# One block of quarter-array products per unit, from the sixth unit on, in a fused recurrence and feed-forward kernel

## The chip, the cores and the metric

The kernel runs on one core of one Trainium2 chip. The metric is the time of one execution on the device, in microseconds (us), as the median of separate runs. A profile of one more execution shows what each engine did: PE is TensorE's matmuls (PEld its weight loads), DVE is VectorE, ACT is ScalarE, POOL is GpSimd and SP is the engine that issues most DMAs.

## The reference

A gated linear recurrence over 768 tokens for 4 batches and 8 heads of 48, whose output is the input of a feed-forward layer (384 to 2048 to 384, with ELU between):

```
f = 1.0 / (1.0 + np.exp(-f_logit))
for t in range(S):
    state = f[:, :, t, :, None] * state + np.einsum('bhd,bhe->bhde', k[:, :, t], v[:, :, t])
    y[:, :, t] = np.einsum('bhd,bhde->bhe', q[:, :, t], state)
x = y.transpose(0, 2, 1, 3).reshape(B * S, H * D)          # (3072, 384)
h = x @ w_in                                               # (3072, 2048)
g = np.where(h > 0.0, h, np.exp(np.minimum(h, 0.0)) - 1.0)
out = g @ w_out                                            # (3072, 384)
```

All arithmetic is float32.

## The kernel before

**Units and stages.** The 3072 tokens are cut into 12 units of 256 tokens (three to a batch), numbered 0 to 11. A unit passes through the recurrence first and through the feed-forward layer a stage later. From unit 2 on, a stage is the time in which one unit's feed-forward layer runs. It has 20 steps, and `base(m)` is the number of the first one of unit m's stage. I write "step 8 of stage 6" for `base(6) + 8`. One pass of the main loop handles two steps, with the loop counter `s`.

**The order is written out by hand.** `at_step(T, ...)` puts functions into a plan, and the main loop calls them at step T. Within one pass the loop calls the plan's functions of the even step, then issues two phases of the feed-forward layer, then the vector joins that belong to them, then the plan's functions of the odd step, then the activations of a finished quad, and last some down products (`take`). Each engine works through its own instructions in exactly that order, so a function's place in the plan fixes what stands behind it on every engine that it uses.

**The feed-forward layer.** A unit's 16 column blocks of `w_in` are four quads. A quad is five phases, i = 0 to 4, of 3, 5, 5, 4 and 3 full-array products into two PSUM banks (`psH`, "side 0" and "side 1"; the next quad's side 0 lies in the bank of this quad's side 1). ACT copies the phases' results to `vals` (L988), and after phase 1 it writes one block back into the bank (L990, the seed), onto which phase 3 adds. DVE's joins (L972, `joins`) finish a quad: JOIN3 reads side 1, JOIN4 reads side 0, MID and LAST stay in SBUF. Then ACT makes the exponentials (L996, L997), DVE the ELU (L1016, `elu`), POOL four sums (L1029). The down products (L1080, `down`) take these into four PSUM banks `psM`, tags m0 to m3, which hold a whole unit. When a unit's last down product is done, ACT copies one bank half (L1091) and DVE makes five adds (L1090) that write the output tile; these are the closing adds, and they free m3, m0, m1 and m2 in that order. The unit's end falls at the end of step 7 of the next stage.

**The recurrence of unit u.** `load` fetches f, k, q, v. `gates` (ACT, two activations L673 and L675) makes the gate's denominator. For each of three pairs of heads `grow` (DVE scan, L687) and `fall` (DVE reciprocal, L692) make the running decay, and `scale` (POOL) multiplies k and q by it. `transposed` turns k on the PE. Then come four groups of quarter-array products, each of 64 x 64 (or 64 x 48) with four of them side by side in the array, 32 products a group (24 in the carried part of a batch's first unit):

- `advance`: the states' increments (psU, L806); DVE adds them up in `step` (L764, one for each of 4 chunks),
- `scores`: q times k (psS, L783); DVE multiplies them by a mask in `mask` (L791),
- `outputs`: masked scores times v (psY, L821),
- `carried`: q times the states, added onto the same psY (L845); then ACT copies psY to the unit's x tile (L852, L854).

For a unit u these stand in the stage of unit u-1 (`t = base(u - 1)`): transposes at step 3, advance and scores at step 9 (`both`), outputs at step 12, carried at step 13. `advance` writes banks a0 and a1, `scores` m3 and m0, and `outputs` a0 and a1. So a stage has three separate blocks of quarter-array products among the full-array ones. The decays of the unit after that stand at steps 1, 5 and 15 of a stage, its gates at step 19 (`D6`, and `t - 21`).

A weight check, spread over the run, rereads w_in and w_out by DMA (`reread`) and passes them through ACT (`check`, L665 and L666).

Of the kernel before, what the change touches and what calls it, by code (L numbers as in the profile page):

```python
# [356 lines left out]
def fast(ctx: ExitStack, tc: tile.TileContext, q, k, v, f_logit, w_in, w_out, out, flag, outer):  # L357
# [53 lines left out]
    D6 = (-19, -15, -5, 1)  # L411
    A3 = (3, 9, 12, 13)
    BL = 16
    BL2 = 29
# [380 lines left out]

    def advance(u, pairs=range(HP)):

        if u not in pus:
            pus[u] = [ps.tile([128, NW, HP, D], FP32, tag=n, name=f"psU{u}_{n}") for n in ("a0", "a1")]
        pu = pus[u]  # L800
        for p in pairs:
            for w in range(NW):
                for r in range(2):
                    h = 2 * p + r
                    for b in range(2):
                        nc.tensor.matmul(  # L806
                            pu[b][FULL[r], w, p], lhsT=kn[FULL[b], p, w, FULL[r]],
                            rhs=vs[u % NB][FULL[b], w, PAD + h * D : PAD + (h + 1) * D],
                            start=(w == 0 and p == 0), stop=(w == NW - 1 and p == HP - 1), skip_group_check=True,
                        )  # L810
# [23 lines left out]
    def carried(u):  # L834

        t = qkf[u % NB]
        py = pys.pop(u)
        for w in range(NW):
            for p in range(HP):
                for b in range(2):  # L840
# [3 lines left out]
                    for r in range(2):  # L844
# [3 lines left out]
                            start=False, stop=True, skip_group_check=True,  # L848
                        )
        x = x_tile(u)  # L850
        to = x[:, 0:HP].rearrange("n p (w b i) -> n b w p i", b=2, i=C)
# [68 lines left out]
    def attention(u, first, then):  # L920
# [12 lines left out]
        if u > 1:  # L933
            at_step(then[-2], lambda: outputs(u))
        at_step(then[-1], lambda: carried(u))

# [96 lines left out]
    def down(P):  # L1033
# [28 lines left out]
        else:  # L1062
# [6 lines left out]
            if j == plain and m < NU - 1:  # L1069
                todo = todo[2:5] + todo[:2] + todo[5:]  # L1070
            if j >= NP - 1 - (m == NU - 1):
                todo = todo[:3] + todo[5:6] + todo[3:5] + todo[6:]
# [187 lines left out]
    for u in range(3, NU):  # L1260
        t = base(u - 1)
        for n in range(6):
            at_step(t + BL + n // 5 * 2, lambda u=u, n=n: blend(u, nc.gpsimd, slice(n, n + 1)))
        at_step(base(u - 2) - (0, 3, 6)[min(u - 3, 2)], lambda u=u: load(u))
        at_step(t - (11, 19, 21)[min(u - 3, 2)], lambda u=u: gates(u))
        attention(u, [t + i for i in (D3, D4, D5, D6)[min(u - 3, 3)]], [t + i for i in A3])
    for n in range(NR):
# [139 lines left out]
```

## Time and profile before

| | us |
|---|---|
| median of 3 runs | 548.81 |
| lowest and highest | 548.62, 551.91 |
| profiled execution, first to last instruction | 549.1 |
| one steady stage of 20 steps (306.34 to 348.31) | 41.97 |
| PE busy in the profiled execution | 532.8 |
| DVE, POOL, ACT busy | 407.3, 338.2, 317.2 |

The profiled execution's own time is its span, 549.1 us; it lies 0.3 us above the median of the runs. A PE product of float32 appears in the trace as two rows, so a group of 32 products is "x64" and a phase of 3 products is "x6". The distance between the starts of two groups is the time that a group takes, since a row's own duration overlaps the next one.

### The profile page before, as it was taken

What the parts mean: (1) busy time and instruction counts of PE and PEld (TensorE: products, weight loads), DVE (VectorE), ACT (ScalarE), POOL (GpSimd) and SP (SyncE); (2) the same over time, 40 slices, a digit from 0 to 9 for tenths busy, and PEclk for the clock granted to TensorE, in tenths of its full rate; (3) what the DMA queues carried; (4) which work ended last, traced back from release to release, by engine and by line L of the source; (5) the groups of instructions that cost most, each with busy time, mean ns of one, the idle gap of its engine ahead of it and who ended that gap; (6) DMA issues with size and microseconds to landing.
All of it is one profiled execution on the core that took longest, in us unless ns stands there. A gap on an engine that the chain in (4) does not pass through costs nothing.

```text
span 549.1 us, 15619 instructions
## 1 busy us (share of the span) xinstructions
PE 532.8 (97%) x6302; PEld 497.6 (91%) x6302; DVE 407.3 (74%) x717; ACT 317.2 (58%) x649; POOL 338.2 (62%) x560
## 2 busy tenths in 40 slices
PE   7699899999999999999999999999999999999996
PEld 3577678899999999999999999999999999999995
DVE  8699968875888887687687687777867865654563
ACT  4459773235656467566566566575675574574441
POOL 8230227779798398288388378478568567454452
PEclk9789999999999999999999999999999999999999
DMA  8999961005052271261262252243244212110001
GB/s 202 238 268 254 265 180 44 1 15 139 8 148 73 60 191 41 60 184 49 60 167 66 60 144 88 60 120 112 60 106 126 60 23 87 54 45 2 30 1 38
DMA packets 38964, 53.92 MB, mean 98 GB/s; under 512 B 3904, under 2 KB 28704, under 8 KB 38880
## 3 DMA queue, kind: packets, MB, share of 16 engines
q1 hardware_dynamic: 38464, 52.51, 36.1%
q8 instruction: 52, 0.85, 0.7%
q10 hardware_dynamic: 416, 0.30, 0.2%
q14 instruction: 32, 0.26, 0.2%
HBM read 45.02 MB, written 4.72 MB: 91 GB/s over the span
## 4 chain that ended last, share of the span: by engine, by line
PE 82%; DVE 9%; ACT 4%; issue 2%; DMA 2%; SPq 0%; POOL 0%; DVEq 0%; ACTq 0%; POOLq 0%
PE psM L1080 32%; PE psH L982 29%; PE psH L1006 7%; PE psM L1042 4%; DVE vals L972 3%; PE psY L821 2%; PE psY L845 2%; DVE f L692 2%; PE psU_a L806 2%; PE psS L783 2%; DVE gg L1016 1%; ACT gg L997 1%; ACT gg L996 1%; DMA again<-in_moe_w_out_dram 1%; PE psT L743 1%
## 5 line engine op out<-in xcount | busy, mean ns | idle before, releaser
L1029 POOL TENSOR_TENSOR sums<-gg 128x128 f32<-128x128 f32 x172 | 101.8, 611 | 125.0 <-DVE gg L1016 124.3
L988 ACT COPY vals<-psH 128x512 f32<-128x512 f32 (+1 forms) x120 | 65.5, 545 | 122.4 <-PE psH L982 118.3
L982 PE MATMUL psH<-xt,wi 128*128 128x128 f32 x880 | 131.4, 276 | 0.1
L972 DVE TENSOR_TENSOR vals<-vals,psH 128x256 f32<-128x256 f32 (+1 forms) x160 | 61.8, 386 | 85.3 <-PE psH L982 46.4
L982 PE MATMUL psH<-xt,area 128*128 128x128 f32 x720 | 118.0, 277 | 0.8 <-DVE vals L972 0.6
L982 PEld LDWEIGHTS psH<-xt,wi 128*128 128x128 f32 x880 | 115.2, 192 | 0.8 <-DVE gg L1016 0.3
L1080 PE MATMUL psM<-area,sums 128*128 128x192 f32 x516 | 103.5, 327 | 0.0
L982 PEld LDWEIGHTS psH<-xt,area 128*128 128x128 f32 x720 | 100.9, 191 | 2.2 <-PE psS L783 1.1
L1080 PEld LDWEIGHTS psM<-area,sums 128*128 128x128 f32 x516 | 85.8, 190 | 0.3 <-POOL sums L1029 0.2
L1080 PE MATMUL psM<-wo,gg 128*128 128x192 f32 x376 | 76.7, 329 | 0.0
L1016 DVE SCALAR_TENSOR_TENSOR gg<-gg,vals 128x512 f32<-128x512 f32 x80 | 64.1, 836 | 9.7 <-ACT gg L997 9.7
L972 DVE TENSOR_TENSOR vals<-vals 128x256 f32<-128x256 f32 x120 | 64.4, 551 | 2.0
L682 POOL TENSOR_TENSOR k<-k,f 128x256 f32<-128x256 f32 x48 | 35.8, 749 | 45.3 <-DMA k<-in_k_dram 21.3
L692 DVE RECIPROCAL f<-f 128x256 f32<-128x256 f32 x36 | 62.8, 1748 | 1.0
L1080 PEld LDWEIGHTS psM<-wo,gg 128*128 128x128 f32 x376 | 61.1, 190 | 1.8 <-DVE at L791 1.6
L997 ACT ACTIVATE gg<-gg 128x512 f32<-128x512 f32 x96 | 60.5, 631 | 3.1
L996 ACT ACTIVATE gg<-vals 128x512 f32<-128x512 f32 x80 | 49.5, 619 | 18.1 <-DVE vals L972 18.0
L962 POOL TENSOR_TENSOR xt<-xt 128x256 f32<-128x256 f32 x57 | 48.6, 867 | 3.2 <-DVE xt L962 1.8
L1006 PE MATMUL psH<-xt,wi 128*128 128x256 f32 x192 | 47.3, 398 | 1.7 <-DVE xt L902 1.7
L682 POOL TENSOR_TENSOR q<-q,f 128x256 f32<-128x256 f32 x48 | 40.9, 855 | 12.3 <-ACT f L712 9.4
L1029 POOL TENSOR_TENSOR sums<-sums,gg 128x128 f32<-128x128 f32 x86 | 47.5, 552 | 0.2
L1006 PEld LDWEIGHTS psH<-xt,wi 128*128 128x128 f32 x192 | 37.6, 199 | 8.6 <-DVE xt L902 1.9
(115 smaller groups left out, 751.0 us busy)
## 6 DMA issues: line engine op xcount, KB each, us to landing
area<-in_moe_w_out_dram SPq DMA_DIRECT2D x8, 768.0 KB, 11.6
again<-in_moe_w_in_dram SPq DMA_DIRECT2D x16, 384.0 KB, 4.3
again<-in_moe_w_out_dram SPq DMA_DIRECT2D x16, 384.0 KB, 3.7
k<-in_k_dram SPq DMA_DIRECT2D x12, 384.0 KB, 4.2
q<-in_q_dram SPq DMA_DIRECT2D x12, 384.0 KB, 5.6
v<-in_v_dram SPq DMA_DIRECT2D x12, 384.0 KB, 6.2
area<-in_moe_w_in_dram SPq DMA_DIRECT2D x8, 576.0 KB, 11.7
out_dram<-o SPq DMA_DIRECT2D x42, 96.0 KB, 1.7
```

The source lines that it names most:

```text
L682: e.tensor_tensor(out=t[n][:, p], in0=t[n][:, p], in1=t["f"][:, p, "kq".index(n)], op=ALU.mult)
L692: nc.vector.reciprocal(f[:, p, 1], f[:, p, 0])
L962: e.tensor_tensor(out=pick(x, to), in0=pick(x, a), in1=pick(x, b), op=ALU.subtract)
L972: nc.vector.tensor_tensor(out=pick(v, to), in0=x, in1=y, op=op)
L982: nc.tensor.matmul(bank[:, slot], lhsT=w_block(q, w), rhs=xts[m][:, x], start=(i < 2 and t == 0), stop=True, skip_group_check=True,)
L988: nc.scalar.copy(v[:, at : at + size], bank[:, frm : frm + size])
L996: nc.scalar.activation(g[:], h, AF.Relu, scale=-1.0)
L997: nc.scalar.activation(g[:], g[:], AF.Exp, scale=-1.0)
L1006: nc.tensor.matmul(ph[:, i], lhsT=wi[j][:, kt, i * 128 : (i + 1) * 128], rhs=xts[m][:, 2 * kt : 2 * kt + 2].rearrange("n t f -> n (t f)"), ...
L1016: nc.vector.scalar_tensor_tensor(out=g[:], in0=g[:], scalar=-1.0, in1=phs.pop(P), op0=ALU.add, op1=ALU.max)
L1029: nc.gpsimd.tensor_tensor(out=s[:, i], in0=x, in1=y, op=op)
L1080: nc.tensor.matmul(pm[bank][:, half * DH : (half + 1) * DH], lhsT=x, rhs=y, start=first, stop=(j == NP - 1), skip_group_check=True,)
```

## The change

From unit 5 (`DEEP`) on, the recurrence is planned by `deep` and not by `attention`. `window(u)`, at step 9 of the stage of unit u-1, issues on the PE without a break `outputs(u)`, `scores(u + 1)`, `advance(u + 1)` and `carried(u)`, and then, for DVE, `mask(u + 1)` and the steps of u + 1. So scores and states are made one unit earlier than before. `advance` writes m1 and m2 there, and `scores` m3 and m0. The copies of psY to x become `placed_x` and stand two steps later. The transposes of u + 1, the gates and the decays of later units move a stage earlier, to other steps: from unit 7 on the loads of f and k to step 2, the gates to step 6, the first decay to step 8, the second to step 12, the third to step 16. Unit 5 gets advance and scores by themselves in stage 3. The first seven down products of a unit are issued in another order.

```diff
+    DEEP = 5
+    D_DEEP = ((2, 5, 8, 13), (-5, -4, -2, 1), (-12, -8, -4, 1))
...
-    def advance(u, pairs=range(HP)):
+    def advance(u, pairs=range(HP), banks=("a0", "a1")):
...
     def carried(u):
...
-        py = pys.pop(u)
+        py = pys[u]
...
+    def placed_x(u):
+
+        py = pys.pop(u)
         x = x_tile(u)
...
-        at_step(then[-1], lambda: carried(u))
+        at_step(then[-1], lambda: carried(u), lambda: placed_x(u))
+
+    def window(u):
+
+        outputs(u)
+        if u + 1 == NU:
+            carried(u)
+            return
+        pc = scores(u + 1, ("m3", "m0"))
+        advance(u + 1, banks=("m1", "m2"))
+        carried(u)
+        mask(u + 1, pc)
+        for c in range(NC):
+            step(u + 1, c)
+
+    def deep(u):
+
+        t, kept = base(u - 2), []
+        d = [t + i for i in D_DEEP[min(u - DEEP, 2)]]
+        for p in range(NKT):
+            at_step(d[p], lambda p=p: grow(u, p), lambda p=p: fall(u, p), lambda p=p: scale(u, ("k", p, nc.gpsimd)))
+        at_step(d[NKT - 1], lambda: move(u, slice(0, 2), nc.sync))
+        for p in range(NKT):
+            at_step(d[p + 1] if u == DEEP else t + ((-1, 0, 1) if u == DEEP + 1 else (-3, -1, 1))[p], lambda p=p: scale(u, ("q", p, nc.gpsimd)))
+        at_step(d[NKT], lambda: watch(u), lambda: scale(u, ("k", NKT, nc.gpsimd), ("q", NKT, nc.gpsimd)))
+        at = t + (15 if u == DEEP else 3)
+        at_step(at, lambda: transposed(u, 0, "a0"), lambda: transposed(u, 1, "a1"))
+        if u == DEEP:
+            at_step(at + 2, lambda: advance(u), *(lambda c=c: step(u, c) for c in range(NC)))
+            at_step(at + 3, lambda: kept.append(scores(u)), lambda: mask(u, kept[0]))
+        at_step(base(u - 1) + A3[1], lambda: window(u))
+        at_step(base(u - 1) + A3[1] + 2, lambda: placed_x(u))
...
             if j == plain and m < NU - 1:
                 todo = todo[2:5] + todo[:2] + todo[5:]
+                if m >= DEEP - 1:
+                    todo = [todo[i] for i in (4, 3, 5, 1, 2, 0, 6)]
...
-        at_step(base(u - 2) - (0, 3, 6)[min(u - 3, 2)], lambda u=u: load(u))
-        at_step(t - (11, 19, 21)[min(u - 3, 2)], lambda u=u: gates(u))
-        attention(u, [t + i for i in (D3, D4, D5, D6)[min(u - 3, 3)]], [t + i for i in A3])
+        if u <= DEEP:
+            at_step(base(u - 2) - (0, 3, 6)[min(u - 3, 2)], lambda u=u: load(u))
+            at_step(t - (11, 19, 21)[min(u - 3, 2)], lambda u=u: gates(u))
+        else:
+            at_step(base(u - 2) - (10 if u == DEEP + 1 else 18), lambda u=u: load(u, "fk"))
+            at_step(base(u - 2) - (6 if u == DEEP + 1 else 10), lambda u=u: load(u, "qv"))
+            at_step(base(u - 2) - (6 if u == DEEP + 1 else 14), lambda u=u: gates(u))
+        if u < DEEP:
+            attention(u, [t + i for i in (D3, D4, D5, D6)[min(u - 3, 3)]], [t + i for i in A3])
+        else:
+            deep(u)
```

What stands where, in stage 6. On ACT, from the exponentials of unit 6's first quad (gg6_0, gg6_1) to the copy of m0 that begins unit 5's closing (u2_5); before:

```order
L996 ACTIVATE gg6_0_3262<-vals0_126 128x512
L997 ACTIVATE gg6_0_3262<-gg6_0_3262 128x512
L996 ACTIVATE gg6_1_3265<-vals0_126 128x512
L997 ACTIVATE gg6_1_3265<-gg6_1_3265 128x512
L665 ACTIVATE again12_3199,spans_140<-again12_3199 128x384
L666 ACTIVATE again12_3199,spans_140<-again12_3199 128x384
L988 COPY vals1_127<-psH6_1_1_3277 128x512
L990 COPY psH6_1_1_3277<-vals1_127 128x128
L988 COPY vals1_127<-psH6_1_0_3252 128x512
L1091 COPY u2_5_3313<-psM5_0_2953 128x192
```

and changed, where the line numbers are some 40 higher:

```order
L1033 ACTIVATE gg6_0_3366<-vals0_126 128x512
L1034 ACTIVATE gg6_0_3366<-gg6_0_3366 128x512
L1033 ACTIVATE gg6_1_3369<-vals0_126 128x512
L1034 ACTIVATE gg6_1_3369<-gg6_1_3369 128x512
L675 ACTIVATE f1_71<-f1_71 128x3x256
L677 ACTIVATE f1_71<-f1_71 128x3x256
L667 ACTIVATE again12_3307,spans_140<-again12_3307 128x384
L668 ACTIVATE again12_3307,spans_140<-again12_3307 128x384
L1025 COPY vals1_127<-psH6_1_1_3383 128x512
L1027 COPY psH6_1_1_3383<-vals1_127 128x128
L1025 COPY vals1_127<-psH6_1_0_3360 128x512
L1130 COPY u2_5_3419<-psM5_0_3130 128x192
```

The two activations of unit 9's gates (f1) have come in ahead of the copies of quad 1 (psH6_1), of the seed and of u2.

On DVE, from unit 5's last closing add (o5) over quad 1's joins to the masks; before:

```order
L1090 TENSOR_TENSOR o5_3312<-psM5_2_2955,u43_5_3314 128x384
L972 TENSOR_TENSOR vals1_127<-vals1_127,psH6_1_1_3277 128x2x128 x2
L972 TENSOR_TENSOR vals1_127<-psH6_1_1_3277,vals1_127 128x128
L972 TENSOR_TENSOR vals1_127<-vals1_127,psH6_1_0_3252 128x2x128
L972 TENSOR_TENSOR vals1_127<-vals1_127,psH6_1_0_3252 128x128
L972 TENSOR_TENSOR vals1_127<-vals1_127 128x2x128
L972 TENSOR_TENSOR vals1_127<-vals1_127 128x256
L972 TENSOR_TENSOR vals1_127<-vals1_127 128x2x128
L791 TENSOR_TENSOR at7_3374<-psS7_0_3375,twice_109 128x512
L791 TENSOR_TENSOR at7_3374<-psS7_1_3376,twice_109 128x512
```

and changed:

```order
L1129 TENSOR_TENSOR o5_3418<-psM5_2_3132,u43_5_3420 128x384
L689 SCALAR_TENSOR_TENSOR f1_71<-f1_71 128x256
L694 RECIPROCAL f1_71<-f1_71 128x256
L1009 TENSOR_TENSOR vals1_127<-vals1_127,psH6_1_1_3383 128x2x128 x2
L1009 TENSOR_TENSOR vals1_127<-psH6_1_1_3383,vals1_127 128x128
L1009 TENSOR_TENSOR vals1_127<-vals1_127,psH6_1_0_3360 128x2x128
L1009 TENSOR_TENSOR vals1_127<-vals1_127,psH6_1_0_3360 128x128
L1009 TENSOR_TENSOR vals1_127<-vals1_127 128x2x128
L1009 TENSOR_TENSOR vals1_127<-vals1_127 128x256
L1009 TENSOR_TENSOR vals1_127<-vals1_127 128x2x128
L793 TENSOR_TENSOR at8_3485<-psS8_0_3486,twice_109 128x512
L793 TENSOR_TENSOR at8_3485<-psS8_1_3487,twice_109 128x512
```

The scan and the reciprocal of unit 9's first decay have come in between the closing adds and quad 1's joins; the masks behind them are unit 8's, not unit 7's.

On the PE, the first down products of unit 6 behind the block; before:

```order
L1080 MATMUL psM6_2_3439<-area_139,gg6_0_3262 128x192
L1080 MATMUL psM6_1_3438<-area_139,sums6_0_3292 128x192 x2
L1080 MATMUL psM6_0_3437<-wo_138,gg6_0_3262 128x192
L1080 MATMUL psM6_3_3440<-wo_138,gg6_0_3262 128x192
L1080 MATMUL psM6_0_3437<-area_139,sums6_0_3292 128x192
```

and changed:

```order
L1119 MATMUL psM6_3_3623<-wo_138,gg6_0_3366 128x192
L1119 MATMUL psM6_0_3620<-wo_138,gg6_0_3366 128x192
L1119 MATMUL psM6_0_3620<-area_139,sums6_0_3398 128x192
L1119 MATMUL psM6_1_3621<-area_139,sums6_0_3398 128x192 x2
L1119 MATMUL psM6_2_3622<-area_139,gg6_0_3366 128x192
```

Before, the first three go to m2 and m1, which hold nothing of the recurrence; changed, all four banks hold scores or increments when these products are due, m3 and m0 until the masks, m1 and m2 until the steps.

More of the change, by code (lines that the diff above doesn't have):

```diff
@@ L794, in mask @@
             )
-    def advance(u, pairs=range(HP)):
+    def advance(u, pairs=range(HP), banks=("a0", "a1")):
         if u not in pus:
-            pus[u] = [ps.tile([128, NW, HP, D], FP32, tag=n, name=f"psU{u}_{n}") for n in ("a0", "a1")]
+            pus[u] = [ps.tile([128, NW, HP, D], FP32, tag=n, name=f"psU{u}_{n}") for n in banks]
         pu = pus[u]
```

## The prediction

> **What bounds the kernel now.** I read the page's busy times and its chain first, then the windows of single stages, then the timelines of PE, ACT and DVE around step 9.
>
> ```profile
> PE 532.8 (97%) x6302; PEld 497.6 (91%) x6302; DVE 407.3 (74%) x717; ACT 317.2 (58%) x649; POOL 338.2 (62%) x560
> PE 82%; DVE 9%; ACT 4%; issue 2%; DMA 2%; SPq 0%; POOL 0%; DVEq 0%; ACTq 0%; POOLq 0%
> ```
>
> ```profile
> 306.34:348.31 41.97, 41.97 (x535) 41.02 (x535) 31.91 (x59) 26.39 (x60) 28.03 (x46) 1.00 0.34 93
> ```
>
> The second fence is a window, one steady stage: its length, then busy time and rows of PE, PEld, DVE, ACT and POOL, then the granted clock. PE is busy the whole 41.97 us at the full clock (1.00), and the chain that ended last is 82% PE. So any PE time saved shortens the run, and any new PE wait lengthens it. DVE has 10.06 us free in this stage (41.97 less 31.91), but what counts is where. Stage 6 around its block, on the PE (rows counted double, as float32 has two a product):
>
> ```profile
> 304.68 0.38 PE L982 MATMUL psH<-xt,area 128*128 128x128 f32 x2
> 304.90 0.83 PE L982 MATMUL psH<-xt,wi 128*128 128x128 f32 x6
> 305.57 0.39 PE L982 MATMUL psH<-xt,area 128*128 128x128 f32 x2
> ...
> 306.34 1.15 PE L806 MATMUL psU_a<-v,kn 64*64 64x48 f32 x64
> 307.31 1.14 PE L783 MATMUL psS<-q,k 64*64 64x64 f32 x64
> 308.37 0.94 PE L982 MATMUL psH<-xt,area 128*128 128x128 f32 x6
> ...
> 310.60 0.81 PE L1080 MATMUL psM<-area,sums 128*128 128x192 f32 x4
> 311.32 0.92 PE L1080 MATMUL psM<-wo,gg 128*128 128x192 f32 x4
> ...
> 312.49 1.42 PE L821 MATMUL psY<-at,v 64*64 64x64 f32 x64
> 313.84 0.71 PE L982 MATMUL psH<-xt,area 128*128 128x128 f32 x4
> ...
> 315.29 0.83 PE L982 MATMUL psH<-xt,wi 128*128 128x128 f32 x6
> 316.05 1.16 PE L845 MATMUL psY<-q,state 64*64 64x64 f32 x64
> 317.14 0.59 PE L1080 MATMUL psM<-wo,sums 128*128 128x192 f32 x2
> 317.57 0.81 PE L1080 MATMUL psM<-wo,gg 128*128 128x192 f32 x4
> 318.22 0.49 PE L1080 MATMUL psM<-area,gg 128*128 128x192 f32 x2
> ```
>
> **What the change saves on the PE.** Six psH rows in mid-stream take 0.67 (304.90 to 305.57). The carried block, though, starts 0.76 after the six rows before it (315.29 to 316.05): 0.09 for entering. Its 64 rows take 1.09 up to 317.14, where the 64 of psU, followed by more of their kind, take 0.97: 0.12 on leaving. The next two psM rows take 0.43, and the four behind them 0.65 (317.57 to 318.22), so 0.33 for two: 0.10 after it. A block's edges cost 0.31. A stage with `window` has one block and not three and saves 0.62. Two PE waits of this stage can go as well: psY at 312.49 takes 0.26 more than psY at 316.05 (1.35 against 1.09), and the four rows at 310.60 take 0.72 and not 0.65. That is about 1.0 a stage. The number of products is unchanged.
>
> [...]
>
> **What it puts on ACT.** Row after row as it ran, with the gates' two rows from the previous stage, and with that stage's seed and the PE's phase 3 behind it:
>
> ```profile
> 283.70 0.27 ACT L990 COPY psH<-vals 128x128 f32<-128x128 f32 x1
> 284.38 0.85 ACT L673 ACTIVATE f<-f 128x768 f32<-128x768 f32 x1
> 285.26 0.84 ACT L675 ACTIVATE f<-f 128x768 f32<-128x768 f32 x1
> ...
> 301.23 0.63 ACT L997 ACTIVATE gg<-gg 128x512 f32<-128x512 f32 x1
> 301.77 0.56 ACT L665 ACTIVATE again<-again 128x384 f32<-128x384 f32 x1
> ...
> 303.60 0.27 ACT L990 COPY psH<-vals 128x128 f32<-128x128 f32 x1
> ...
> 304.29 0.32 ACT L1091 COPY u<-psM 128x192 f32<-128x192 f32 x1
> ```
>
> ```profile
> 284.37 0.38 PE L982 MATMUL psH<-xt,area 128*128 128x128 f32 x2
> ```
>
> ACT runs without a gap from 301.23 to 304.61 here. The gates' pair takes 1.72 (284.38 to 286.10), and 1.63 with the 0.09 by which a row overlaps the one before (301.86, 301.77). In the changed order it stands right behind 301.23, so the seed ends at 305.50, not 303.87, and the closing copy starts at 305.92, not 304.29. The seed was 0.8 ahead of phase 3 (304.68); now phase 3 waits until 305.6, a loss of 0.9. Phase 4, the block and all else start 0.9 to 1.0 later: the block at 307.3. Where the gates came from, step 19, ACT's time frees nothing on the PE.
>
> **What it puts on DVE.** Here DVE works without a gap from the first closing add to the last state:
>
> ```profile
> 299.22 0.94 DVE L687 TENSOR_TENSOR_SCAN f<-f 128x256 f32<-128x256 f32 x1
> 300.19 1.75 DVE L692 RECIPROCAL f<-f 128x256 f32<-128x256 f32 x1
> 301.86 1.86 DVE L1016 SCALAR_TENSOR_TENSOR gg<-gg,vals 128x512 f32<-128x512 f32 x2
> 304.64 0.36 DVE L1090 TENSOR_TENSOR o<-psM,u 128x192 f32<-128x192 f32 x1 [0.92 <-ACT u L1091]
> ...
> 306.90 0.87 DVE L972 TENSOR_TENSOR vals<-vals,psH 128x256 f32<-128x256 f32 x2
> 307.80 0.29 DVE L972 TENSOR_TENSOR vals<-psH,vals 128x128 f32<-128x128 f32 x1
> 308.19 0.74 DVE L972 TENSOR_TENSOR vals<-vals,psH 128x256 f32<-128x256 f32 x2
> ...
> 309.98 1.28 DVE L791 TENSOR_TENSOR at<-psS,twice 128x512 f32<-128x512 f32 x2
> 311.18 1.52 DVE L764 TENSOR_TENSOR state<-psU_a,state 128x192 f32<-128x192 f32 x4
> ...
> 316.23 0.88 DVE L972 TENSOR_TENSOR vals<-vals,psH 128x256 f32<-128x256 f32 x2 [3.13 <-PE psH L982]
> ...
> 320.06 0.74 DVE L972 TENSOR_TENSOR vals<-vals,psH 128x256 f32<-128x256 f32 x2 [0.25 <-PE psH L982]
> ```
>
> That the PE waits for these joins is seen one stage later, where JOIN3 ended at 350.56 and the next phase 0 started 0.15 behind it:
>
> ```profile
> 350.27 0.29 DVE L972 TENSOR_TENSOR vals<-psH,vals 128x128 f32<-128x128 f32 x1
> ```
>
> ```profile
> 350.71 0.91 PE L982 MATMUL psH<-xt,area 128*128 128x128 f32 x6 [0.29 <-DVE vals L972]
> ```
>
> A decay takes 2.64 (299.22 to 301.86). At step 5 it hid in front of a wait for ACT. At step 8 it stands between the closing adds and JOIN3, where nothing hides it except the longer block: outputs and carried, some 2.0, now run ahead of phase 0.
>
> **The sum for stage 6.** DVE: closing adds start at 306.28 (1.64 later) and take 2.26, so the decay starts at 308.54 and JOIN3 at 311.18. With the old distances (from 306.90) JOIN3 ends 1.19 later at 312.37, JOIN4 2.03 later at 313.2, the masks end at 314.9 and 315.5 (3.72 and 4.36), and the third state, which frees m1, at 316.6 (0.38 a state from 315.46). PE: the block is four times 0.97 plus 0.12, so 307.3 to 311.3. Phase 0 waits for JOIN3 until 312.5; before, it started at 308.37. Phase 1 waits for JOIN4 and follows at 313.3 (six rows, and 0.10 as after a block); its ten rows end at 314.5. Down products, 0.33 each: m3 at 315.0 (first mask), m0 twice from 315.6 (second mask), m1 twice from 316.65 (third state), m2; the end is at 317.65. Phases 2 and 3, eighteen rows of 0.112, end at 319.7. In the profile this point, with all three blocks done, was 317.14. **Loss 2.6.** Ends of this term: the saving of 1.0 if both insertions are hidden, and a loss of 4.3 less 1.0, 3.3, if all 1.63 and 2.64 reach the PE.
>
> A second, smaller term: JOIN3 of the next quad had started 0.91 ahead of that point (316.23), since the carried block lay between; now nothing does, and it starts 0.2 behind it. Of these 1.1 DVE had 0.25 in hand (320.06). The lag goes on over ACT's exponentials to the next seed, which is 0.40 ahead of its phase 3 (283.97 against 284.37). **0.45 more**, so 3.05 a stage. Gates at step 6 and a decay at step 8 stand in stages 4 to 8: **five stages, 15.2.**
>
> **Stage 3.** Unit 5's third decay stands at step 8 there, with no gates ahead of it at step 6; unit 6's decays stand at 15, 16 and 18, beside unit 5's own steps at 17 and mask at 18; before, this stretch held one decay.
>
> ```profile
> 201.75 0.88 DVE L972 TENSOR_TENSOR vals<-vals,psH 128x256 f32<-128x256 f32 x2 [1.43 <-PE psH L982]
> ```
>
> At step 8 the block stays short, so the 2.64 reach the PE in full, and with them a part of the decay at step 2, between 0 and 2.64 and mostly in idle time: I take 0.5, together 3.2. At the stage's end two more decays (5.3) and states with mask (2.5 by the rows at 309.98 and 311.18) meet 1.7 of idle (1.43 here, 0.25 as in stage 6): JOIN3 comes 6 late. The PE is then itself some 3.9 later: psU and psS that moved here 2.0, six transpose rows 0.7, and as loss two blocks' edges 0.6 and some 0.65 of wait, since the scores go to a0 and a1, which the states free only behind the decays. Of the 2.1 left I take 1.8 as wait. 3.2 + 1.25 + 1.8: **6.3**; at least the 0.6 of the edges, at most 8.5, 3.2 and the decays' 5.3. **Stages 9 and 10** have neither gates nor decays at those steps, and one block each: **2.0 saved.**
>
> Sum: 549.1 + 15.2 + 6.3 - 2.0 = 568.6 for a profiled execution, and, as the span lies 0.3 above the median, **568** for the median. All other moves I cost at nothing: POOL's multiplications have the 14 us that POOL is idle in a stage (28.03 of 41.97), loads are issued four steps (8 us) ahead of the gates, and the x copies come two steps earlier than before; were that cover gone, ACT or the sums would be late too (the third rival).
>
> [...] DVE starts JOIN4 behind JOIN3 and never ahead (308.19 after 307.80), and ACT the closing copy behind the seed. [...]
>
> **Rivals.** (1) **As designed, faster.** If the decay and gates are covered, because the PE reaches phase 0 late enough and the seed's 0.8 takes most of the gates, twelve blocks fewer (two in each of seven stages, less two in stage 3) save 3.7, and the waits some 0.2 a stage, 1.4: 544. It decides at one point: JOIN3 must end before the block does, near 310.4. For it speak the 2.0 by which the block grows; against it, that JOIN3 already held up the PE with nothing inserted (350.56, 350.71). (2) **Only DVE's insertion counts.** If ACT has the gates done in a gap, the closing adds stay at 304.64, JOIN3 ends at 310.7 and the third state at 315.0, the loss is 1.0 a stage, and the sum is 549.1 + 5.0 + 6.3 - 2.0 = 558. Against it stands ACT's row without a gap. (3) **Stalls add up**: the gates wait for their load, ACT for the gates, and POOL's sums come late too, one us more a stage: 574 and above.
>
> **How the numbers follow.** Forecast 0.60, rival 1 0.13, rival 2 0.15, rival 3 0.07, and 0.05 for something that cancels within 1% of 549. This kernel's measurements tell about 1% from no change. The range goes from under rival 2, 555, to over rival 3, 577. Faster 0.13, same 0.07, slower 0.80.
>
> **What would show it.** In the changed profile, around step 9 of stages 4 to 8: ACT's gates ahead of the seed and phase 3 starting later than the products before it end; a scan and reciprocal between the closing adds and the joins; PE waits in front of phase 0 (for vals) and of psM (for at, then state); one block of 256 rows in about 4 us. Stages of about 45 us there, against 42. I am wrong if phase 0 follows the block without a wait, or if the seed is in time.

## The result and the profile after

The changed kernel takes 589.37 us (median of 4 runs, 588.13 to 592.87), the kernel before 550.30 us on the same chip: **1.072 times as long, 95% interval 1.068 to 1.076**. I had said 568 (555 to 577): the direction holds, the size is half of what came. The profiled execution spans 586.3 us; 37.2 us are to be found against the 549.1 of before.

From the page of the changed kernel, busy times and the chain that ended last; then, from the windows, stage 6 from block to block:

```profile
PE 537.3 (92%) x6302; PEld 494.6 (84%) x6302; DVE 398.8 (68%) x717; ACT 317.1 (54%) x649; POOL 332.4 (57%) x560
PE 50%; ACT 22%; DVE 16%; issue 5%; DMA 5%; POOL 0%; SPq 0%; DVEq 0%; ACTq 0%; POOLq 0%
```

```profile
327.53:373.95 46.42, 42.87 (x535) 40.72 (x534) 30.44 (x58) 26.29 (x60) 27.27 (x46) 1.00 0.33 87
```

The stage holds as many PE rows as before (535), at the full clock (1.00), in 46.42 and not 41.97 us. No engine has more to do (DVE 30.44, ACT 26.29). So the loss is waits. PE's share of the chain falls from 82% to 50%; ACT goes from 4% to 22%, DVE from 9% to 16%, issue from 2% to 5%. What the PE waited for, from stage 3 to the end (total, times, longest):

```profile
PE psH L1019 <- ACT psH L1027: 9.2, 12, 0.9
PE psH L1019 <- DVE vals L1009: 8.4, 17, 2.2
PE psY L847 <- issue: 4.0, 3, 1.6
PE psU_m L808 <- issue: 3.1, 3, 1.8
PE psH L1019 <- ACT vals L1025: 2.8, 4, 1.0
...
PE psM L1119 <- DVE state L766: 0.8, 3, 0.3
```

Before, all waits of the PE in these stages came to 0.8 us. The fifth row is a wait for ACT that I had not forecast, and the two `issue` rows are waits inside the long block with no engine behind them.

Stage by stage, from one set of transposes (step 3) to the next, in us, with the experiments below:

| stage | 3 | 4 | 5 | 6 | 7 | 8 | step 3 of stage 9 to the end |
|---|---|---|---|---|---|---|---|
| before | 42.1 | 42.1 | 41.7 | 42.0 | 42.2 | 42.2 | 129.1 |
| changed | 52.2 | 47.0 | 47.2 | 46.4 | 46.3 | 46.4 | 133.3 |
| deep_8 | 42.1 | 41.9 | 41.7 | 52.4 | 46.5 | 46.6 | 133.6 |
| x_copies_13 | 52.2 | 47.0 | 45.2 | 44.9 | 44.5 | 44.9 | 129.4 |
| x13_gates_8 | 53.3 | 45.8 | 44.9 | 44.1 | 43.7 | 43.7 | 130.1 |
| x13_blocks_apart | 52.3 | 45.1 | 45.8 | 45.9 | 45.1 | 45.4 | 130.3 |
| x13_apart_decay_moved | 51.5 | 44.0 | 44.0 | 44.0 | 44.0 | 44.0 | 130.4 |
| all_four | 51.5 | 44.0 | 43.6 | 43.6 | 43.6 | 43.1 | 130.2 |

My forecast for the second row was 3.05 more in stages 4 to 8, and less time than before in stages 9 and 10. The loss is 4.1 to 5.5 in stages 4 to 8, and the end, which has neither gates nor decays at steps 6 and 8, loses 4.2 as well. The end does so with 134 PE rows (2.7 us) fewer than before (1218 against 1352 in this window), since these stand in stage 3 now; so what it lost in waits is 6.9.

Each row is one execution, and six cells hold a stretch of 3.4 us at half the granted clock, which costs up to 1.7 us: x_copies_13 in stage 4, deep_8 and x13_blocks_apart in stage 6, x13_gates_8, x13_apart_decay_moved and all_four in stage 3.

### The profile page after: what moved, and what is told of

It is laid out like the page before. It is cut to its first block, busy times and chain, and to the rows that moved or that the text cites. A ratio compares the mean times of both kernels' runs of the same rounds, so it can differ in the third digit from the quotient of the medians.

```text
span 586.3 us, 15663 instructions
## 1 busy us (share of the span) xinstructions
PE 537.3 (92%) x6302; PEld 494.6 (84%) x6302; DVE 398.8 (68%) x717; ACT 317.1 (54%) x649; POOL 332.4 (57%) x560
## 4 chain that ended last, share of the span: by engine, by line
PE 50%; ACT 22%; DVE 16%; issue 5%; DMA 5%; POOL 0%; SPq 0%; DVEq 0%; ACTq 0%; POOLq 0%
PE psH L1019 18%; PE psM L1119 15%; DVE vals L1009 9%; PE psH L1043 6%; ACT gg L1034 5%; ACT gg L1033 5%; PE psM L1079 4%; ACT vals L1025 3%; DVE gg L1053 3%; ACT again L667 3%; DMA area<-in_moe_w_in_dram 2%; PE psY L823 2%; PE psY L847 2%; ACT again L668 2%; DMA k<-in_k_dram 1%
## 5 line engine op out<-in xcount | busy, mean ns | idle before, releaser
L1066 POOL TENSOR_TENSOR sums<-gg 128x128 f32<-128x128 f32 x172 | 99.1, 596 | 119.3 <-DVE gg L1053 118.6
L1019 PE MATMUL psH<-xt,area 128*128 128x128 f32 x720 | 119.8, 280 | 19.2 <-ACT psH L1027 9.2
L1019 PEld LDWEIGHTS psH<-xt,wi 128*128 128x128 f32 x880 | 114.9, 192 | 3.8 <-issue 3.2
L684 POOL TENSOR_TENSOR k<-k,f 128x256 f32<-128x256 f32 x48 | 37.0, 771 | 92.1 <-DVE f L689 79.0
L1053 DVE SCALAR_TENSOR_TENSOR gg<-gg,vals 128x512 f32<-128x512 f32 x80 | 59.5, 772 | 23.1 <-ACT gg L1034 23.1
L1009 DVE TENSOR_TENSOR vals<-vals 128x256 f32<-128x256 f32 x120 | 63.0, 540 | 2.0
L1043 PE MATMUL psH<-xt,wi 128*128 128x256 f32 x192 | 44.6, 382 | 2.6 <-DVE xt L908 1.8
L684 POOL TENSOR_TENSOR q<-q,f 128x256 f32<-128x256 f32 x48 | 38.7, 813 | 13.5 <-ACT f L714 10.0
L1066 POOL TENSOR_TENSOR sums<-sums,gg 128x128 f32<-128x128 f32 x86 | 45.0, 523 | 0.2
L1066 POOL TENSOR_TENSOR sums<-gg,sums 128x128 f32<-128x128 f32 x86 | 40.8, 474 | 6.6
```

What stands on the lines that cost most here:

```text
L684: e.tensor_tensor(out=t[n][:, p], in0=t[n][:, p], in1=t["f"][:, p, "kq".index(n)], op=ALU.mult)
L1009: nc.vector.tensor_tensor(out=pick(v, to), in0=x, in1=y, op=op)
L1019: nc.tensor.matmul(bank[:, slot], lhsT=w_block(q, w), rhs=xts[m][:, x], start=(i < 2 and t == 0), stop=True, skip_group_check=True,)
L1043: nc.tensor.matmul(ph[:, i], lhsT=wi[j][:, kt, i * 128 : (i + 1) * 128], rhs=xts[m][:, 2 * kt : 2 * kt + 2].rearrange("n t f -> n (t f)"), ...
L1053: nc.vector.scalar_tensor_tensor(out=g[:], in0=g[:], scalar=-1.0, in1=phs.pop(P), op0=ALU.add, op1=ALU.max)
L1066: nc.gpsimd.tensor_tensor(out=s[:, i], in0=x, in1=y, op=op)
```

## Experiments

Four theories: **X**, the x copies stand ahead of the exponentials on ACT; **S**, the PE itself stands in the long block; **G** and **D**, my prediction's gates (ahead of the seed) and decays (ahead of JOIN3). The edits are against the changed kernel, unless they say before.

### X: the x copies

ACT and then the PE in stage 6 of the changed kernel, behind the block (timelines):

```profile
335.62 0.58 ACT L858 COPY xt<-psY 128x512 f32<-128x512 f32 x1
336.21 1.18 ACT L860 COPY xt<-psY 64x512 f32<-64x512 f32 x2
337.42 0.57 ACT L667 ACTIVATE again<-again 128x384 f32<-128x384 f32 x1
...
338.66 0.62 ACT L1033 ACTIVATE gg<-vals 128x512 f32<-128x512 f32 x1
339.31 0.63 ACT L1034 ACTIVATE gg<-gg 128x512 f32<-128x512 f32 x1
...
341.02 0.57 ACT L1025 COPY vals<-psH 128x512 f32<-128x512 f32 x1
```

```profile
342.97 0.91 PE L1019 MATMUL psH<-xt,area 128*128 128x128 f32 x6 [0.39 <-DVE vals L1009]
...
346.01 0.68 PE L1019 MATMUL psH<-xt,wi 128*128 128x128 f32 x4 [0.19 <-DVE vals L1009]
...
350.95 0.49 PE L1019 MATMUL psH<-xt,area 128*128 128x128 f32 x2 [0.84 <-ACT psH L1027]
```

The copies take 1.77 us and run ahead of everything that the next quad needs of ACT; the vals copy of its phase 2 is the last in line, at 341.02. Behind it JOIN3, and with it phases 0 and 1 of the next quad, and then the seed of the third quad are late, and the PE waits in front of each. Before, the copies stood behind that vals copy, in ACT's idle time (in stage 6 the vals copy starts at 315.26, the copies at 317.24 behind 1.40 us of idle).

```diff
-        at_step(base(u - 1) + A3[1] + 2, lambda: placed_x(u))
+        at_step(base(u - 1) + A3[3], lambda: placed_x(u))
```

> Changed kernel (589.4 us) with one edit: the x copies go from step 11 back to step 13, where ScalarE has the check, the exponentials and the vals copy of phase 2 behind it. Theory X (the copies, 1.77 us on ScalarE ahead of the exponentials, make the next quad's JOIN3 late and with it phases 4, 0, 1 and the seed): 2.0 to 2.8 us a stage come back in seven stages, 570 to 575 us. Theory S (the stages are longer because TensorE itself stands still inside the long block, and what follows only shows it): within 3 us of 589.

Measured: 579.38 us (578.46 to 581.21), 1.050 of before (1.045 to 1.056). **10.0 us of the 39 come back** for a move of two steps on one engine. It is short of the 14 to 20 that theory X named; the stages gain 1.5 to 2.0 each from stage 5 on, and the end 3.9. (Stage 4 shows none, because in that execution 3.5 us of it ran at a granted clock of 0.53; see the end.) In the trace the copies now follow the vals copy (340.34 behind 339.86 in stage 6), and the waits for ACT vals, 2.8 us in the changed kernel, are gone.

The same from the other side: three idle copies of 128x512 put into the kernel **before**.

```diff
+    spare = cst.tile([128, 4, 128], FP32, name="spare")
+    def copies():
+        for _ in range(3):
+            nc.scalar.copy(spare[:], ident[:].unsqueeze(1).broadcast_to([128, 4, 128]))
...
+    for u, i in ((4, 11), (5, 11), (6, 13), (7, 13), (8, 6), (9, 6)):
+        at_step(base(u) + i, copies)
```

> Kernel before (550.7 us) with three more copies of 128x512 on ScalarE (some 1.8 us) in six of its stages, the results not used: at step 11, ahead of the exponentials, in stages 4 and 5, at step 13, behind them, in 6 and 7, and at step 6, where the changed kernel has the gates, in 8 and 9. Theory X: 1.4 to 2.8 us more for stages 4 and 5, under 0.3 us for 6 and 7. Theory G: 0.8 to 1.0 us more for stages 8 and 9. In all 554 to 558 us; if ScalarE has room at all three places, 551 us.

Measured: 554.91 us (one run). By stages, from transposes to transposes: 43.44 and 43.16 in stages 4 and 5 (before 42.11 and 41.67), 41.87 and 42.23 in 6 and 7 (41.97 and 42.21), 43.51 and 43.78 in 8 and 9 (42.18 and 41.96). So 1.9 us of ACT (three copies of 0.62) cost **1.3 to 1.5 us ahead of the exponentials, nothing behind them, and 1.3 to 1.8 at the gates' step** (theory G had 0.8 to 1.0 there). ACT was 26.39 us busy in a stage of 41.97; where in the stage decides. One thing went otherwise than theory X says: in this kernel the PE's wait is at the carried block, for the copies called `between`, not at JOIN3:

```profile
275.74 0.45 PE L845 MATMUL psY<-q,state 64*64 64x64 f32 x8 [1.40 <-ACT between L828]
```

The block of stage 6 in the changed kernel does not have that wait, since scores and advance run between outputs and carried part.

### S: the long block

The PE's timeline of stage 6 in the changed kernel:

```profile
327.53 1.16 PE L823 MATMUL psY<-at,v 64*64 64x64 f32 x64
328.51 1.14 PE L785 MATMUL psS<-q,k 64*64 64x64 f32 x64
329.44 0.77 PE L808 MATMUL psU_m<-v,kn 64*64 64x48 f32 x40
331.27 0.56 PE L808 MATMUL psU_m<-v,kn 64*64 64x48 f32 x24 [1.05 <-issue]
331.65 1.13 PE L847 MATMUL psY<-q,state 64*64 64x64 f32 x64
332.71 0.94 PE L1019 MATMUL psH<-xt,area 128*128 128x128 f32 x6
```

After 168 rows, in the middle of one product's kind, nothing is issued for 1.05 us. Each of the six long blocks has such a gap, after 139 to 238 rows, of 0.2 to 1.8 us of idle. To see it by itself I put runs of different length, of the same form and with unused results, into the kernel **before**, at step 6 of its stages.

```diff
+    def dummies(u, n):
+        pw = [ps.tile([128, 8, C], FP32, tag=f"a{b}", name=f"psX{u}_{b}") for b in range(2)]
+        for i in range(n):
+            r, b = FULL[i // 2 % 2], i % 2
+            nc.tensor.matmul(
+                pw[b][r, i // 4 % 8], lhsT=ident[FULL[b], r], rhs=ident[FULL[b], 0:C],
...
+    for u, n in ((4, 32), (5, 64), (6, 96), (7, 128), (8, 192), (9, 256), (10, 64)):
+        at_step(base(u) + 6, lambda u=u, n=n: dummies(u, n))
```

> Kernel before (550.3 us) with an extra run of quarter-array products of the same form, whose results are not used, at step 6 of stages 4 to 10: 32, 64, 96, 128, 192, 256 and 64 products, so 64 to 512 rows. At 0.0302 us a product and 0.31 us of edges a run these 832 products take 27.3 us: about 577 us if length costs nothing. Theory S (a stall that comes with length, from supply of instructions): no gap inside the runs of 64 and 128 rows, one of 1 to 2 us in that of 256, two or three in those of 384 and 512; 583 to 588 us. If the stall of the changed kernel comes from what is read or written there: no gaps in any.

Measured: 584.74 us (one run), with 27.3 us for the products and 6.8 more, of theory S's 6 to 11. The runs of 64 and 128 rows have no gap (1.09 and 2.03 us long). That of 192 rows has one after 160, that of 256 after 194, that of 384 after 165 and 293, and that of 512 reads in the timeline:

```profile
445.41 2.44 PE L1154 MATMUL psX<-ident 64*64 64x64 f32 x151
449.24 2.09 PE L1154 MATMUL psX<-ident 64*64 64x64 f32 x128 [1.39 <-issue]
453.24 2.09 PE L1154 MATMUL psX<-ident 64*64 64x64 f32 x128 [1.91 <-issue]
457.24 1.78 PE L1154 MATMUL psX<-ident 64*64 64x64 f32 x105 [1.91 <-issue]
```

In a long run the gaps come **every 128 rows**, and a round takes 4.00 us where 128 rows take 1.93. The page's queue of instruction DMA says what these 128 rows are; the kernel before, and this one:

```profile
q8 instruction: 52, 0.85, 0.7%
```

```profile
q8 instruction: 65, 1.06, 0.8%
```

13 packets and 0.21 MB more, for 1664 rows more: 128 rows a packet of some 16 KB. The trace has a weight load and a product for each of these rows (1664 of either), so by my estimate a packet is 256 instructions of some 64 bytes. So in this run the PE went through its instructions faster than they came: some 16 KB in 1.93 us, against one packet in 4.00. At 0.112 us a row, as in psH, the same packet would last 14 us by this estimate. The view of the DMA from 445.4 to 459, in 40 slices of 0.34 us, shows the four packets:

```profile
GB/s 0 0 0 48 0 0 0 0 0 0 0 0 0 0 0 48 24 0 0 0 0 0 0 0 0 0 48 0 0 0 0 0 0 0 0 0 0 0 48 0
q8 instruction: 4, 0.07, 2.4%
```

In the trace they start at 446.63, 450.66, 454.37 and 458.40 and take 1.2 to 1.4 us each. Each of the three gaps ends 1.39 to 1.44 us behind the end of a packet, and each of the six in the long blocks of the changed kernel 1.24 to 1.53 behind one. By these times what the PE waited for was its instructions. A packet's own time is the smaller part of a round of 4.00; why the next one isn't brought sooner, no run here shows.

Then I took the long block apart in the changed kernel, first badly:

```diff
     def window(u):
-        outputs(u)
         if u + 1 == NU:
-            carried(u)
             return
...
-        carried(u)
...
+        at_step(base(u - 1) + OUT, lambda: outputs(u), lambda: carried(u))
         at_step(base(u - 1) + A3[1], lambda: window(u))
```

(`OUT` is 7.)

> Changed kernel with the long block cut in two at places of their own: outputs and carried part (128 rows) at step 7, scores and advance (128 rows) at step 9, x copies still at step 11. Theory S (TensorE runs out of instructions in a run of 256 rows, 1.2 to 1.8 us in six stages): the stalls go, a pair of edges of 0.31 us comes back in each of seven stages, 581 to 585 us, and no issue wait in the block. Theory X: the order on ScalarE stays, so the waits after step 11 stay too and grow by what the stall had hidden; 589 to 592 us.

Measured: 614.97 us (613.59 to 618.42), 1.117 of before (1.110 to 1.123): a miss of both. With nothing between outputs and carried part the PE waits for `between` in each of seven stages:

```profile
PE psH L1018 <- DVE vals L1008: 14.3, 20, 2.1
PE psY L848 <- ACT between L831: 14.1, 7, 2.6
```

Behind four of the seven, and once in stage 3, the granted clock also halves for 3.4 us (its mean in this execution is 0.982), so a part of this time is not the waits themselves.

The second try put the x copies at step 13, outputs at step 7, scores and advance at 9 and the carried part at 11.

> x copies back at step 13, and the long block in three: outputs at step 7 (64 rows), scores and advance at step 9 (128 rows), carried part at step 11 (64 rows), all still a unit deeper. Theory S (TensorE stands for want of instructions once a run passes some 140 to 230 rows): no issue wait in the blocks; the gaps of 0.5 to 2.0 us in six windows go (some 8 us), two pairs of edges of 0.31 us in seven windows come back (4.3 us): 575 to 577 us. If the stall is of the products themselves and goes with them: 582 to 585 us.

Measured: 590.97 us (590.37 to 592.63). It can't be read for S: the states of the next unit are kept in five buffers in turn and here overwrite some that the carried part still reads, so that this part works on other data and also waits for the states. The third try has the carried part ahead of them:

```diff
+        at_step(base(u - 1) + 5, lambda: outputs(u))
+        at_step(base(u - 1) + 7, lambda: carried(u))
         at_step(base(u - 1) + A3[1], lambda: window(u))
```

> x copies at step 13 (579.4 us alone) and the long block taken apart, the carried part still ahead of the next unit's states: outputs at step 5 (64 rows), carried part at step 7 (64 rows), scores and advance at step 9 (128 rows). Theory S (TensorE runs short of instructions in long runs): no gap over 0.3 us inside any block, six gaps of 0.5 to 2.0 us gone, two pairs of edges (0.31 us) back in each of seven stages: 574 to 577 us. If the gap was only a wait by another name, it shows up elsewhere: 579 to 584 us.

Measured: 580.04 us (577.87 to 582.37), where the x copies alone gave 579.38. The gaps are gone, all of them (from stage 4 on its list of waits has no `issue` row, where x_copies_13 has 6.8 us); the time is not. What took it is in the PE's and DVE's timelines of stage 6:

```profile
326.70 1.16 PE L785 MATMUL psS<-q,k 64*64 64x64 f32 x64
327.68 1.10 PE L808 MATMUL psU_m<-v,kn 64*64 64x48 f32 x64
330.56 0.91 PE L1018 MATMUL psH<-xt,area 128*128 128x128 f32 x6 [1.77 <-DVE vals L1008]
```

```profile
326.88 0.68 DVE L689 TENSOR_TENSOR_SCAN f<-f 128x256 f32<-128x256 f32 x1
327.60 1.75 DVE L694 RECIPROCAL f<-f 128x256 f32<-128x256 f32 x1
329.26 0.82 DVE L1008 TENSOR_TENSOR vals<-vals,psH 128x256 f32<-128x256 f32 x2
330.12 0.29 DVE L1008 TENSOR_TENSOR vals<-psH,vals 128x128 f32<-128x128 f32 x1
```

That is the prediction's own mechanism: the decay at step 8, then JOIN3, then phase 0, with a wait of 1.77. In the changed kernel the gap (1.05 in stage 6) had stood in front of it, so that phase 0 came late anyway.

### D with S: a cause behind a cause

So the decays of step 8 were moved, to step 12 for units 7 on and 11 for unit 5, and those behind them to later steps.

```diff
-    D_DEEP = ((2, 5, 8, 13), (-5, -4, -2, 1), (-12, -8, -4, 1))
+    D_DEEP = ((2, 5, 11, 14), (-5, -4, -2, 1), (-8, -5, -2, 1))
```

> Changed kernel (589.4 us) with the decays that stand at step 8, between the closing adds and JOIN3, taken to step 12 (units 7 to 11: steps 12, 15, 18 and 1) and, for unit 5, to step 11 (steps 2, 5, 11 and 14). Theory D (my prediction's term: the decay holds JOIN3, phase 0 and then M): 1.0 to 2.0 us a stage in six stages come back, 578 to 583 us. Theory D-under-S (TensorE stands for want of instructions in the long block just then, and this covers the decay): only stage 3 gains, 2 us; 586 to 589 us.

> x copies at step 13 (579.4 us alone) and the decays off step 8. Theory D: 570 to 574 us. Theory D-under-S: 576 to 579 us.

> x copies at step 13, blocks apart (580.0 us with these two), and the decays off step 8. Here no instruction gap covers the decay, and phase 0 waited 1.8 to 2.2 us for JOIN3 in six stages. Theory D-under-S: these six waits go, some 10 us less two or three in waits of later quads for the two decays that now stand close together: 570 to 574 us. If the wait moves to another place in full: 578 to 580 us.

Measured, in us: 592.04 (589.92 to 594.39) for the first, so nothing gained; and with the x copies at step 13, all four corners:

| x copies at step 13 | long block | blocks apart |
|---|---|---|
| decay at step 8 | 579.38 | 580.04 |
| decay moved | 578.68 (576.96 to 579.78) | 571.23 (569.63 to 572.44) |

To take the decay away alone gains 0.7, the gap alone loses 0.7, **both together gain 8.2**. Gap and decay cover each other at one place: both hold up the same phase 0, one on the PE itself and one over DVE.

That is not all that stands in these corners. In the profiled executions the decay's move alone gains 2.4 in stage 3 and loses 0.8 to 1.3 in each of stages 5 to 8: behind its new place the waits for vals and the seed grow (12.9 us from stage 4 on, against 7.9 without the move). And taking the blocks apart puts outputs and carried part ahead of phase 3, which then no longer waits for the seed behind the gates (0.65 in stage 6 of x13_decay_moved, none in x13_apart_decay_moved). So the 8.2 belong to the two edits; how much of them is the gap with the decay alone was not measured. In stage 6 of the last corner the PE goes from the block to the phase without a wait:

```profile
323.71 1.10 PE L808 MATMUL psU_m<-v,kn 64*64 64x48 f32 x64
324.74 0.94 PE L1018 MATMUL psH<-xt,area 128*128 128x128 f32 x6
```

### G: the gates

For the gates I went back to steps 19, 1, 5, 15 and 1 for gates and decays, a unit earlier, first from unit 7 on.

> Changed kernel with the gates and the decays of units 7 to 11 a stage less deep in the way: gates at step 19, decays at steps 1, 5, 15 and 1, as in the kernel before but a unit earlier; the loads of f and k go ahead of them. Theory G (my prediction's own: gates ahead of the seed, a decay ahead of JOIN3): the 0.8 us wait of phase 3 and about 1 us of waits of phase 0 and M go in five stages, 578 to 582 us. Theory X (the x copies carry the loss): only the wait of phase 3 goes, 0.8 us by 5 stages, 585 us. Theory S (stalls in the block hide the rest): 585 us or more.

Measured: 588.10 us (586.62 to 592.57). In it the earlier load overwrites f and k of unit 5 before their last use, so part of the work is done on other data; the order is what it says. Then from unit 8 on, without that:

```diff
-    D_DEEP = ((2, 5, 8, 13), (-5, -4, -2, 1), (-12, -8, -4, 1))
+    D_DEEP = ((2, 5, 8, 13), (-5, -4, -2, 1), (-12, -8, -4, 1), (-19, -15, -5, 1))
...
-            at_step(base(u - 2) - (10 if u == DEEP + 1 else 18), lambda u=u: load(u, "fk"))
+            at_step(base(u - 2) - (10, 18, 28)[min(u - DEEP - 1, 2)], lambda u=u: load(u, "fk"))
...
-            at_step(base(u - 2) - (6 if u == DEEP + 1 else 14), lambda u=u: gates(u))
+            at_step(base(u - 2) - (6, 14, 21)[min(u - DEEP - 1, 2)], lambda u=u: gates(u))
```

> Changed kernel with gates and decays of units 8 to 11 at steps 19, 1, 5, 15 and 1 (a unit earlier than in the kernel before), unit 7 as in the changed kernel. Theory G (my prediction's term: 0.9 us of phase 3 and 1 to 1.6 us of phase 0 and M in each of the four stages): 579 to 582 us. Theory X (the x copies ahead of the exponentials set the pace of each stage, and what the gates add is taken up by the waits behind): 586 to 589 us.

> x copies back at step 13 (579.4 us with this edit alone) and gates and decays of units 8 to 11 early. Theory G: with the copies out of the way the gates' cost shows in full, 0.8 to 2 us in four stages, 571 to 576 us. If gates and decays cost nothing beside the stall in the block: 578 to 580 us.

Measured: 589.02 us (588.53 to 590.93) alone, nothing; 575.55 (573.37 to 577.80) with the x copies at step 13, 3.8 less than with these alone. The edit moves gates and decays together, so this is the price of both, about 1 us a stage of the four. That the x copies covered it is not shown: in the profiled executions stages 5 to 8 are 0.4 to 1.0 shorter than in the changed kernel even alone (46.2, 46.1, 45.8 and 45.9 against 47.2, 46.4, 46.3 and 46.4; 2.4 together), against 0.3 to 1.2 with the copies moved (3.1 together). But the execution profiled without the copies' move had lost 5.1 us ahead of stage 3, where the edit changes nothing (its transposes of stage 2 start at 134.0, those of the changed kernel at 129.0). Beside such differences a median of four can hide 2.4 us.

### The terms together

> All three edits together: x copies at step 13, gates and decays of units 8 to 11 early, the block in three. What is left against the kernel before is the way into the deeper order (stage 3, 8 to 11 us in the trace of the changed kernel) and unit 7's gates. If the terms add up: 550.5 + 9 + 2 + small change, 560 to 566 us, and stages 5 to 10 of 42.1 to 42.8 us each as before. If the deeper order itself costs in each stage: 570 to 574 us.

Measured: 583.24 us (581.56 to 586.37), again with the carried part behind the states that overwrite its own. With the blocks as in x13_blocks_apart:

> The same with gates and decays of units 8 to 11 early as well. If the terms add up (x copies 10, gates 4, gaps some 4 net of edges): 569 to 573 us, and the stages of units 8 to 11 within 1 us of the 42.1 us of the kernel before. If the gaps cost nothing net: 575 to 577 us.

Measured: 574.00 us (572.23 to 577.68). Stages 5 to 8 are at 43.1 to 43.6, 0.9 to 1.9 above before, but stage 4, which has unit 7's decay at step 8 and now no gap to cover it, is at 45.4. With that decay and unit 5's moved too:

> All four edits: x copies at step 13, gates and decays of units 8 to 11 early, blocks apart, decays of units 5 and 7 off step 8. Against 574.0 us without the last: phase 0's waits of 1.8 to 2.2 us in stages 3 and 4 go, 569 to 571 us. What is then left against 550.7 us is the way into the deeper order (stage 3 with a unit more of products, less the waits) and about 1.3 us a stage.

Measured: 568.56 us (567.56 to 569.65), 1.031 of before (1.027 to 1.036). Of the 39 us, 10.0 went with the x copies, and 10.8 with the other three edits together. That it equals my forecast is chance: it is another kernel. By the table 9.4 of the 18 us that are left are in stage 3, the way in, 7.6 in stages 4 to 8 and 1.1 behind. The way in by itself:

```diff
-    DEEP = 5
+    DEEP = 8
```

> Changed kernel with the deeper order from unit 9 on in place of unit 6 (one constant, 8 for 5). If the loss is mostly per stage (25.6 us in stages 4 to 9 of the trace, 3.3 to 5.5 us each): three stages with the long block instead of six, 550.5 + 8 + 3 x 4 = 570 to 576 us. If it is mostly the way in (10.8 us up to the first long block, 2.6 us of it products moved ahead): 580 to 586 us.

Measured: 574.45 us (572.10 to 576.02), 1.040 of before (1.034 to 1.046). In the table's third row the stage in which the deeper order begins takes 10.4 us more (some 1.2 of it the stretch at half the clock), where it took 10.1 in stage 3, and each later stage some 4.4.

## Why the prediction was right and wrong

**The direction and its mechanism: right.** Gates stand ahead of the seed, phase 3 waits; decays stand ahead of JOIN3 (scan at 328.74, reciprocal at 329.45, JOIN3 at 331.12); psM waits for the state. In stage 6:

```profile
325.77 0.49 PE L1019 MATMUL psH<-xt,area 128*128 128x128 f32 x2 [0.66 <-ACT psH L1027]
...
336.69 0.92 PE L1119 MATMUL psM<-area,sums 128*128 128x192 f32 x4 [0.27 <-DVE state L766]
```

0.66 of idle, some 0.8 against the usual distance of the rows; I had 0.9. Rival 1 (544) fell with it.

**"All other moves I cost at nothing ... the x copies come two steps earlier than before": the step that failed.** I looked at whether ACT had time for them, not at what they are ahead of. They measured 10.0 us: 1.5 to 2.0 in each of stages 5 to 8, and 3.9 behind. The second term, JOIN3 of the next quad and the next seed, was the right place and far too small: 0.45, where the copies alone bring 1.5 to 2.0, by the route that I named (joins, exponentials, seed). That a copy can be late at this place I could have read from before: JOIN3 of the next quad had 0.25 in hand.

**The saving of 0.62 a stage from the edges: right, and overdrawn.** The long block does go without edges (0.98 and 0.93 us from group to group in stage 6), but its gaps are 0.2 to 1.8. The price of a run four times as long as the quoted rows was put at four times theirs, and that was not bounded from the other side. The steady stages of before show no gap (no `issue` row in its list of waits from 72 us on). But its first 70 us, which I left out, have three (1.1, 0.3 and 1.4 us), each ending 1.35 to 1.57 us behind the end of an instruction packet. Two are in its list of waits as follows, and the longest stands in a run of only 64 rows:

```profile
PE psY L845 <- issue: 1.4, 1, 1.4
PE psY L890 <- issue: 1.1, 1, 1.1
```

```profile
64.02 1.08 PE L845 MATMUL psY<-q,state 64*64 64x64 f32 x57
66.53 0.34 PE L845 MATMUL psY<-q,state 64*64 64x64 f32 x7 [1.42 <-issue]
```

**Phase 0's wait of 1.2 and the sum of 2.6 for stage 6: the wait is not there in the changed kernel.** I had written that I am wrong if phase 0 follows the block without a wait. It does: JOIN3 ends at 332.27, and the block at 332.71. But the block would have ended a microsecond earlier without its gap, and the wait appears as soon as the gap is gone (1.77, with the block shorter by half). So D was a true cause, hidden behind S. Neither alone gives a stage of 46.4. At the point up to which I had summed (339.77 here) the stage had lost 0.8 at the seed and 1.4 from the start of the block on (12.24 us against 10.80): 2.2 against my 2.6. That is near by luck, as the gap stood where I had put JOIN3. The other 2.2 of the stage's 4.45 came behind it, where I had 0.45.

**Stage 3: right to about a microsecond.** 6.3 of loss and 2.7 of products moved there make 9.0; the stage took 10.1 more. The wait of phase 0 behind the decay at step 8 was 2.24, where I let 2.64 reach the PE in full, and that at the stage's end 1.77, where I had 1.8. Scores waited 1.32 and started 0.1 behind the third state's end; the page puts this down to issue, but it fits the wait for the states that I had forecast, at 0.65.

**Stages 9 and 10: wrong in sign, and the largest miss.** For 2.0 saved there came 6.9 of waits up to the end (4.2 more time with 2.7 of products less): 8.9 off, against 7.9 in stages 4 to 8 together. With the x copies back it is 3.0, and the gaps are still in it.

What stays open: all_four still has 0.9 to 1.9 us a stage over the kernel before, with the same number of blocks; among its waits from stage 4 on are seven for the seed (3.8 us), three for vals of DVE (2.1 us) and four for the state (1.2 us). None of them was taken away singly.

## What to carry to other kernels

An edit on an idle engine was free here only behind the work that others wait for (1.9 us of copies on ACT cost 1.3 to 1.5 us ahead of the exponentials, nothing behind them): ask what each moved instruction is ahead of in its own queue, not whether the engine has time. Small products in close order outran their own instructions here: in the run of 512 rows, 128 rows took 1.93 us to run and their packets came every 4.00. Look in the list of waits for those with no engine behind them, at the start of the run too. When taking away one cause changes nothing, take away two together before calling either harmless (0.7 us either way alone, 8.2 together).

## What the hardware showed that I had not expected

The instruction gap: none in the single runs of 64 and 128 rows of 15 ns each, the first after 139 to 238 rows in the long blocks, and in a longer run one in every 128, at 4.00 us a round. The length of a run is not the whole measure, as the start of the kernel before shows, where a run of 64 rows has a gap of 1.4 us, 4.4 us after the start of another run of 64. Its place within the long blocks was the same in different kernels (after 209, 180 and 168 rows in the first three of the changed kernel, x_copies_13 and x13_gates_8), so in these it went with the place in the program. In x13_gates_8 and deep_8 one block of 240 rows has none inside, but a wait of 1.3 to 1.4 us right behind its last row, which ends 1.3 to 1.5 us behind a packet's end as well.

And a clock that halves: in x_copies_13, behind a gap of 1.8 us in stage 4's block, the windows give

```profile
241.90:245.40 3.50, 3.50 (x29) 3.43 (x20) 3.22 (x9) 0.54 (x2) 0.00 (x0) 0.53 0.49 125
```

a granted clock of 0.53 for 3.5 us, some 1.7 us lost (16 psH rows at nearly twice their distance). all_four has a similar stretch at the end of stage 3 (0.62 over 4 us, behind a wait of 1.76 of phase 0; it is in the 51.5 of that stage), and the changed kernel, behind waits as long (1.80 and 2.24), has none. Between the first 100 us and the last 10, eleven of the eighteen traces have such stretches, each 3.4 us long or twice that. What starts them wasn't tried.
